# Attention and two mixtures of experts in one program: zero rows and expert weights issued at other steps, a first routing group of five tiles, k in 2 KB pieces, gates and domain probabilities made in the first mixture

## The chip, the cores and the metric

One Trainium2 chip, of which one core runs the whole program in a single launch. The core has five engines that run side by side, each with its own queue in order: TensorE (PE in the profile, PEld its weight loads), VectorE (DVE), ScalarE (ACT), GpSimd (POOL) and SyncE (SP), which here only issues DMAs. The metric is the device time of one execution in microseconds, lower is better. TensorE's granted clock in the profile is a share of 2.4 GHz, and 0.50 means 1.2 GHz.

## The reference, cut to what matters

```python
# attention: 4 batches, 8 heads, 576 positions, 64 wide; window of 128, linear bias by distance
scores = scale * np.matmul(q, k.transpose(0, 1, 3, 2))
scores = np.where((rel >= 0) & (rel < 128), scores + bias, -1e9)
attn = softmax(scores)                       # + 1e-9 in the denominator
x = (attn @ v) as 2304 rows of 512
# first mixture: 8 experts, each row goes to its best one alone
logits = x @ w_gate; e = argmax(logits)
gate = softmax(logits)[e]                    # + 1e-9 in the denominator
x = gate * (relu(x @ w1[e]) @ w2[e])
# second mixture: 4 domains, each row goes through all of them
p = domain_probs / (domain_probs.sum(-1) + 1e-9)
out = sum over e of p[:, e] * (relu(x @ w1[e]) @ w2[e])
```

## The kernel before, in words

The 2304 rows are 18 tiles of 128. Three stages follow one another: attention, the first mixture (one expert after the other, on the rows sorted by expert) and the second mixture (three passes over four domains). Nothing is scheduled by a planner: each engine's queue has the order in which the Python code is written.

**Attention** is a loop over 36 steps `s`, two per tile `t` (four heads each). It is a software pipeline: step `s` issues the scores of step s (`st_qk`, L419), the mask and maximum (`st_max`, on DVE), the exponentials of s-1 (`st_exp`, on ACT), the transposes of s-2 (`st_turn`, L463, copied out by ACT on L465), and the products with v of s-3 (`st_pv`, L486). Between the copy and the products POOL cuts each transposed block in two with two selects (L472): one for the tile's own keys and one for the tile before. `st_row` divides by the denominators on DVE and gives the finished rows `xrow` and the logits. The first steps of some tiles also turn a batch of v against the gate weights (`st_gates`, L554), which waits for `rvt`, v in transposed form.

**Routing** is done for groups of tiles (`CUTS`: 0-2, 3-5, 6-8, 9-11, 12-13, 14-15, 16, 17). When the last tile of a group is finished, the generator `st_route` takes the maximum, the one-hot choice `oh_all`, the rank of each row in its expert (matmuls into `rkp`, L630 to L636), and then one indirect DMA per tile on POOL's queue (L664), which scatters the rows into the DRAM table `xs`, at the place of their expert. `route_op` issues one operation of it at a time, three or four calls a step.

The table must be zero where no row lands. `clear_rows(e)` (L318) therefore writes 384 rows of zeros (768 KB) for each of the 8 experts, in the steps 2 to 9. A scatter can reach any of the 8 regions, so the first scatter waits for all of them.

**SP's queue** carries nearly all loads of this stage in one order: k, q and v of the next tiles (256 KB each; k and q three tiles ahead, v one), `rvt` in batches, the zero rows, and `raw`, the first weights of the first mixture (512 KB each). Six of these weights are already split into a high and a low part here (`w_split`: ACT makes `whi`, L146, and in the next step DVE makes `wlo`, L150), in the steps of `SPLITS`. The k tile in SBUF has the layout head pair, slot, column, so that one k tile lands in pieces of 512 bytes.

**Gates.** For all groups below `OPEN` (tile 14) the gate of each row is worked out beside the routing in attention (`gate_of`: a subtraction, an exponential on ACT, a sum, an addition, a reciprocal); for the last four tiles it is done in the first mixture by `places`, a generator that advances by one operation after each of the mixture's units from the second expert on. Its last product is `ct`, a table that the second mixture reads first. `domain_probs` (L389 to L392, four DVE operations) runs at step 20.

Of the kernel before, what the change touches and what calls it, by code (L numbers as in the profile page):

```python
# [19 lines left out]
P = 128  # L20
# [13 lines left out]
CUTS = 0, 3, 6, 9, 12, 14, 16, 17, 18  # L34
# [4 lines left out]
SPLITS = 6, 11, 16, 21, 26, 31  # L39
# [23 lines left out]
def kernel(  # L63
# [40 lines left out]
    lgl = const.tile([P, NTT - OPEN, E1], F32, tag="lgl", name="lgl")  # L104
    mxl = const.tile([P, NTT - OPEN, 1], F32, tag="mxl", name="mxl")
    shl = const.tile([P, NTT - OPEN, E1], F32, tag="shl", name="shl")
# [98 lines left out]
    def gate_of(t0, lg, mx, sh, apart=1):  # L205
        m = lg.shape[1]
        gs = gs_all[:, t0:t0 + m]
        nc.vector.tensor_tensor(out=sh, in0=lg, in1=mx.to_broadcast([P, m, E1]), op=ALU.subtract)
        for _ in range(apart):
            yield  # L210
        nc.scalar.activation(out=sh, in_=sh, func=AF.Exp)
        yield
        nc.vector.tensor_reduce(out=gs, in_=sh, axis=AX.X, op=ALU.add)
        yield
        nc.vector.tensor_scalar(out=gs, in0=gs, scalar1=1e-9, scalar2=None, op0=ALU.add)
        yield
        nc.vector.reciprocal(out=gs, in_=gs)
        yield

    def attention():  # L220
        actx = ExitStack()
        with actx:
# [12 lines left out]
            kr = c2.tile([P, NP, NK, P], F32, tag="kr", name="kr")  # L235
# [89 lines left out]
            dpt = c2.tile([P, N // P, E2], F32, tag="dpt", name="dpt")  # L325


# [11 lines left out]
            def row_consts():  # L339
                nc.sync.dma_start(out=dpt, in_=dp)  # L340
# [46 lines left out]
            def domain_probs():  # L387
                dsum = c2.tile([P, N // P, 1], F32, tag="dsum", name="dsum")
                nc.vector.tensor_reduce(out=dsum, in_=dpt, axis=AX.X, op=ALU.add)  # L389
                nc.vector.tensor_scalar(out=dsum, in0=dsum, scalar1=1e-9, scalar2=None, op0=ALU.add)  # L390
                nc.vector.reciprocal(out=dsum, in_=dsum)
                nc.vector.tensor_tensor(  # L392
                    out=pn, in0=dpt, in1=dsum.to_broadcast([P, N // P, E2]), op=ALU.mult
                )


# [13 lines left out]
            def st_qk(s):  # L410
                t, hf = divmod(s, 2)
                keys, sl = geom(t)
                w = len(keys) * P
                ps = ps_s.tile([P, 2, 2, 2 * P], F32, tag="sc", name=f"sc{s}")
                for jj in range(2):
                    j = 2 * hf + jj
                    for r in range(2):
                        rows = slice(r * D, (r + 1) * D)
                        nc.tensor.matmul(  # L419
                            ps[:, r, jj, 0:w], qs[t][rows, j, :], kr[rows, j, sl, :], start=True, stop=True  # L420
                        )
                sc[s] = ps
# [73 lines left out]
            def st_row(s):  # L496
# [3 lines left out]
                if hf == 0 and t < LATE:  # L500
                    rowt[t] = xpool.tile([P, H, D], F32, tag="row", name=f"xrow{t}", bufs=6)
# [80 lines left out]
            def st_logits(t):  # L582
                g = group_of[t]
                if t == groups[g][0]:
                    if t < OPEN:
                        lgs[g] = route.tile([P, len(groups[g]), E1], F32, tag="lg", name=f"lg{g}")
                    else:
                        lgs[g] = lgl[:, t - OPEN:t - OPEN + len(groups[g])]
# [5 lines left out]

            gates = []

            def st_route(g):
# [8 lines left out]
                mx = t3("mx", 1) if t0 < OPEN else mxl[:, t0 - OPEN:t0 - OPEN + m]  # L606
# [4 lines left out]
                if t0 < OPEN:  # L611
                    gates.append((g, gate_of(groups[g][0], lg, mx, t3("sh"), 4)))
# [130 lines left out]

            for s in range(ns):
# [4 lines left out]
                keep = st_gates(s - 2) if s == 2 else None  # L749
                closing = s == 2 * LATE + 3  # L750
# [19 lines left out]
                if s == 2:  # L770
                    nc.vector.tensor_tensor(
                        out=least, in0=fac, in1=small_of.to_broadcast([P, PER, H]), op=ALU.mult
                    )
                    st_vw(0)
                    st_last(0)
# [36 lines left out]
                while s == 2 * LATE + 2 and not waiting:  # L812
# [5 lines left out]
            for _, steps in gates:  # L818
                for _ in steps:
                    pass  # L820
# [14 lines left out]
    def moe():  # L835
        mctx = ExitStack()
        with mctx:
# [81 lines left out]
            def first_mixture():  # L919
                pctx = ExitStack()  # L920
                with pctx:
# [248 lines left out]

                    def places():
# [7 lines left out]
                        yield from gate_of(OPEN, lgl, mxl, shl)  # L1179
# [313 lines left out]
```

## Time and profile before

| what | time |
|---|---|
| three runs | 1143.1, 1146.97 and 1145.77 us, median 1145.77 us |
| the profiled execution | 1142.88 us |
| span of its instructions | 1141.2 us |
| TensorE busy in the span | 1122.5 us (98%) |
| VectorE, ScalarE, GpSimd busy | 764.6, 516.3, 117.4 us |
| mean granted clock | 0.996 |

The span begins and ends with TensorE's program, and the 1.7 us around it are start and end of the execution. A busy TensorE is not one at its peak: within attention its matmuls take turns with weight loads. So the time is read by stages. Step 0 of attention begins at 6.51 us of the span, step 35 at 135.69 us; the first matmul of the first mixture stands at 153.57 us.

### The profile page before, as it was taken

How to read it: one execution, taken by the hardware profiler on the slowest of the kernel's cores; microseconds unless marked ns; L12 is line 12 of the kernel's file. 1: busy time of each engine (PE TensorE's matmuls, PEld its weight loads, DVE VectorE, ACT ScalarE, POOL GpSimd, SP SyncE). 2: the span in 40 equal slices, each digit the busy share in tenths (PEclk: the TensorE clock that was granted, in tenths of full speed). 3: DMA queues.
4: the chain of work that ended last, by engine and by line, in shares of the span. 5: the costliest groups of instructions: out<-in, count | busy, mean ns of one | idle time of the engine just before them, and what ended most of it. 6: DMA issues, size and time to landing. Idle time of an engine off the chain costs nothing.

```text
span 1141.2 us, 17166 instructions
## 1 busy us (share of the span) xinstructions
PE 1122.5 (98%) x6490; PEld 1024.0 (90%) x6490; DVE 764.6 (67%) x1424; ACT 516.3 (45%) x1006; POOL 117.4 (10%) x192
## 2 busy tenths in 40 slices
PE   9899999999999999999999999999999999999997
PEld 6687889999999989999999999999999999999996
DVE  7778864645754686766667866666677966666663
ACT  6677734544654443344434433333334543433331
POOL 4444520012200000000000300000001100000002
PEclk9999999999999999999999999999999999999999
DMA  9966244555654122222121322211222312122201
GB/s 318 356 213 195 85 150 159 193 162 161 201 195 131 57 78 72 74 74 74 56 74 57 130 74 74 74 57 55 74 75 86 105 68 64 66 74 74 75 19 55
DMA packets 68941, 126.52 MB, mean 111 GB/s; under 512 B 26080, under 2 KB 35296, under 8 KB 68832
## 3 DMA queue, kind: packets, MB, share of 16 engines
q1 hardware_dynamic: 64544, 113.91, 31.1%
q0 software_dynamic: 3456, 9.51, 2.1%
q8 instruction: 76, 1.25, 0.4%
q10 hardware_dynamic: 832, 1.57, 0.4%
q14 instruction: 33, 0.27, 0.1%
HBM read 109.18 MB, written 15.80 MB: 110 GB/s over the span
## 4 chain that ended last, share of the span: by engine, by line
issue 71%; PE 12%; POOL 2%; POOLq 0%
PE y L972 6%; PE g L867 6%; POOL out_dram L1424 2%; PE xps L939 1%; POOLq L1489 0%; POOLq L1424 0%
## 5 line engine op out<-in xcount | busy, mean ns | idle before, releaser
L150 DVE TENSOR_TENSOR wlo<-raw,whi 128x1024 fp32r<-128x1024 f32 x160 | 193.7, 1223 | 128.9 <-ACT whi L146 127.5
L146 ACT CAST whi<-raw 128x1024 fp32r<-128x1024 f32 x160 | 165.7, 1055 | 134.2 <-DVE raw L172 111.1
L1399 PE MATMUL l<-whi,hlo 128*128 128x512 f32 x576 | 224.6, 390 | 0.0
L1399 PE MATMUL l<-wlo,hhi 128*128 128x512 f32 x576 | 224.5, 390 | 0.0
L1399 PE MATMUL l<-whi,hhi 128*128 128x512 f32 x576 | 224.0, 389 | 0.0
L1303 ACT COPY x<-X 128x384 f32<-128x384 f32 x126 | 60.7, 482 | 267.0 <-PE X L1282 267.0
L1420 DVE SCALAR_TENSOR_TENSOR acc<-l,ct,acc 128x512 f32<-128x512 f32 x126 | 94.2, 748 | 85.4 <-PE l L1399 85.4
L1399 PEld LDWEIGHTS l<-whi,hlo 128*128 128x128 f32 x576 | 108.1, 188 | 22.5
L1399 PEld LDWEIGHTS l<-wlo,hhi 128*128 128x128 f32 x576 | 108.1, 188 | 22.0
L1399 PEld LDWEIGHTS l<-whi,hhi 128*128 128x128 f32 x576 | 108.1, 188 | 21.9
L1424 POOL DMA_INDIRECT out_dram<-acc,ctok x18 | 23.3, 1294 | 812.5 <-DVE acc L1420 485.2
L1308 DVE TENSOR_TENSOR x<-Z,x 128x384 f32<-128x384 f32 x84 | 44.7, 553 | 67.6 <-ACT x L1303 67.6
L1314 ACT ACTIVATE hhi<-x 128x384 fp32r<-128x384 f32 x126 | 58.1, 521 | 30.9 <-DVE x L1308 30.9
L486 PE MATMUL xo<-vr,pt 128*128 128x104 f32 x448 | 66.2, 280 | 5.6 <-POOL pt L472 4.9
L972 PE MATMUL y<-hhi,whi 128*128 128x256 f32 (+2 forms) x224 | 69.5, 310 | 0.0
L972 PE MATMUL y<-hlo,whi 128*128 128x256 f32 (+2 forms) x224 | 69.0, 308 | 0.0
L972 PE MATMUL y<-hhi,wlo 128*128 128x256 f32 (+2 forms) x224 | 68.8, 307 | 0.0
L486 PEld LDWEIGHTS xo<-vr,pt 128*128 128x128 f32 x448 | 57.9, 194 | 10.7 <-POOL pt L472 6.4
L1320 DVE SCALAR_TENSOR_TENSOR hlo<-x,hhi 128x384 fp32r<-128x384 f32 x126 | 62.8, 553 | 2.8 <-ACT hhi L1314 0.2
L854 ACT ACTIVATE hhi<-g 128x384 fp32r<-128x384 f32 x64 | 31.3, 493 | 48.8 <-PE g L867 45.0
L855 DVE SCALAR_TENSOR_TENSOR hlo<-g,hhi 128x384 fp32r<-128x384 f32 x64 | 35.1, 554 | 26.7 <-ACT hhi L854 25.2
L472 POOL TENSOR_SCALAR_AFFINE_SELECT pt<-pt 128x512 f32<-128x512 f32 x64 | 40.9, 664 | 64.8 <-ACT pt L465 58.5
(362 smaller groups left out, 2496.9 us busy)
## 6 DMA issues: line engine op xcount, KB each, us to landing
raw<-in_w_b_dram SPq DMA_DIRECT2D x96, 512.0 KB, 3.4
raw<-in_w_a_dram SPq DMA_DIRECT2D x64, 512.0 KB, 3.7
xs<-zrow SPq DMA_DIRECT2D x8, 768.0 KB, 8.3
kr<-in_k_dram SPq DMA_DIRECT2D x18, 256.0 KB, 4.2
v<-in_v_dram SPq DMA_DIRECT2D x18, 256.0 KB, 5.2
row<-xs SPq DMA_DIRECT2D x6, 768.0 KB, 5.6
rq<-in_q_dram SPq DMA_DIRECT2D x16, 256.0 KB, 4.3
rvt<-in_vt_dram SPq DMA_DIRECT2D x3, 1024.0 KB
```

What stands on the lines that cost most here:

```text
L146: nc.scalar.copy(out=hi, in_=src)
L150: nc.vector.tensor_tensor(out=lo, in0=src, in1=hi.bitcast(F32), op=ALU.subtract)
L486: nc.tensor.matmul(xo[:, i, :], pt[c][:, i, :], rows[c % NV][:, h * span:h * span + WIDE], start=(n == 0), stop=(n == len(pt) - 1),)
L867: nc.tensor.matmul(ps[:, 0:w], wl[:, c0:c0 + P], xl[dt // 2][:, dt % 2, 0:w], start=(dt == 0 and n == 0), stop=(dt == NDT - 1 and n == 2),)
L972: nc.tensor.matmul(acc[:, 0:w], wl[:, c0:c0 + P], hl[:, 0:w], start=(f == 0 and x == 0), stop=(f == NFT - 1 and x == 2),)
L1303: nc.scalar.copy(out=to, in_=xb[i])
L1308: nc.vector.tensor_tensor(out=c, in0=ps, in1=c, op=ALU.add)
L1314: nc.scalar.activation(out=hi, in_=c, func=AF.Relu)
L1320: nc.vector.scalar_tensor_tensor(out=lo, in0=c, scalar=0.0, in1=hi.bitcast(F32), op0=ALU.max, op1=ALU.subtract)
L1399: nc.tensor.matmul(acc, hl[:, ts], wl[:, c0:c0 + DM], start=(m == 0 and x == 0), stop=(m == 3 and x == 2),)
L1420: nc.vector.scalar_tensor_tensor(out=accs[g], in0=acc, scalar=pe, in1=accs[g], op0=ALU.mult, op1=ALU.add)
L1424: nc.gpsimd.indirect_dma_start(out=outv[g], out_offset=bass.IndirectOffsetOnAxis(ap=ctok[:, g, :], axis=0), in_=accs.pop(g), in_offset=Non ...
```

## The change

The parts: `clear_rows` runs in the steps 2, 3, 5, 6, 8, 9, 11 and 12; the two weight loads of the steps 3 and 5 go to 10 and 12, and the six splits from the steps 6, 11, 16, 21, 26, 31 to 13, 16, 19, 22, 25, 28. The groups become 0-4, 5-7, 8-10, 11-12, 13-14, 15, 16, 17. The k tile's slot becomes the outer axis, so that a k tile lands in pieces of 2 KB. All gates and the domain probabilities are made in `places`. The gate columns of v of tile 0 (`st_vw(0)`) are issued after the scores of step 3.

```diff
-CUTS = 0, 3, 6, 9, 12, 14, 16, 17, 18
+CUTS = 0, 5, 8, 11, 13, 15, 16, 17, 18
-SPLITS = 6, 11, 16, 21, 26, 31
+SPLITS = 13, 16, 19, 22, 25, 28
-    lgl = const.tile([P, NTT - OPEN, E1], F32, tag="lgl", name="lgl")
+    lgl = const.tile([P, NTT, E1], F32, tag="lgl", name="lgl")
...
-    def gate_of(t0, lg, mx, sh, apart=1):
+    def gate_values():
+        gs, sh = gs_all, lgl
+        nc.vector.tensor_tensor(out=sh, in0=lgl, in1=mxl.to_broadcast([P, NTT, E1]), op=ALU.subtract)
+        yield
         nc.scalar.activation(out=sh, in_=sh, func=AF.Exp)
...
-            kr = c2.tile([P, NP, NK, P], F32, tag="kr", name="kr")
+            kr = c2.tile([P, NK, NP, P], F32, tag="kr", name="kr")
...
-                nc.sync.dma_start(out=kr[:, :, t % NK, :], in_=k[t])
+                nc.sync.dma_start(out=kr[:, t % NK], in_=k[t])
...
-                    rowt[t] = xpool.tile([P, H, D], F32, tag="row", name=f"xrow{t}", bufs=6)
+                    rowt[t] = xpool.tile([P, H, D], F32, tag="row", name=f"xrow{t}", bufs=8)
...
             def route_op(head=False):
-                if gates and not head and (waiting or not back):
-                    if next(gates[0][1], "end") == "end":
-                        gates.pop(0)
-                elif back and (head or not waiting):
+                if back and (head or not waiting):
...
+            clears = [2 + 3 * e // 2 for e in range(E1)]
             for s in range(ns):
...
+                if s == 3:
+                    st_vw(0)
+                    st_last(0)
...
-                if s in (3, 5):
+                if s in (SPLITS[0] - 3, SPLITS[0] - 1):
                     w_dma(nxt["dma"])
-                if 2 <= s < E1 + 2:
-                    clear_rows(s - 2)
-                if s == 20:
-                    domain_probs()
+                if s in clears:
+                    clear_rows(clears.index(s))
...
-                while s == 2 * LATE + 2 and not waiting:
+                while s >= 2 * LATE and back and not waiting:
                     route_op()
...
-                        yield from gate_of(OPEN, lgl, mxl, shl)
+                        yield from domain_probs()
+                        yield from gate_values()
```

Three places in the engines' queues show it. The first is where SP issues the last zero rows, and the loads in front of them. Before (`zrow` is the source of the zero rows, `rvt8` the batch of v from tile 8 on, the number of `rq` the tile):

```order
L318 DMA xs_69<-zrow_162 384x1x512
L258 DMA rvt8_693<-in_vt_dram 128x4x512
L318 DMA xs_69<-zrow_162 384x1x512
L249 DMA v1_0_126<-in_v_dram 128x8x64
L244 DMA kr_119<-in_k_dram 128x4x128
L245 DMA rq8_753<-in_q_dram 128x512
```

Now:

```order
L242 DMA rq8_717<-in_q_dram 128x512
L133 DMA raw0_720<-in_w_a_dram 128x1024
L315 DMA xs_69<-zrow_161 384x1x512
L246 DMA v1_1_126<-in_v_dram 128x8x64
L241 DMA kr_118<-in_k_dram 128x512
L242 DMA rq9_820<-in_q_dram 128x512
L133 DMA raw1_823<-in_w_a_dram 128x1024
L315 DMA xs_69<-zrow_161 384x1x512
```

The last zero rows stood before the q of tile 8 and stand now behind that of tile 9 and two weights.

The second is POOL's first scatter; `pt9` are the selects of step 9's probabilities, which step 11 issues. Before:

```order
L472 AFFINE_SELECT pt8_1_722<-pt8_718 128x512
L440 MEMSET pr11_762 128x4x64
L472 AFFINE_SELECT pt9_0_780<-pt9_778 128x512
L472 AFFINE_SELECT pt9_1_782<-pt9_778 128x512
L664 DMA xs_69<-xrow0_361,row_i_76 18433x512
L472 AFFINE_SELECT pt10_0_834<-pt10_832 128x512
```

Now:

```order
L456 AFFINE_SELECT pt12_1_902<-pt12_898 128x512
L456 AFFINE_SELECT pt13_0_963<-pt13_961 128x512
L456 AFFINE_SELECT pt13_1_965<-pt13_961 128x512
L641 DMA xs_69<-xrow0_359,row_i_76 18433x512
L456 AFFINE_SELECT pt14_0_1011<-pt14_1009 128x512
```

The first scatter moved four steps down POOL's queue.

The third is the end of POOL's queue in attention; the number of `xrow` is the tile. Before:

```order
L664 DMA xs_69<-xrow13_1776,row_i_76 18433x512
L472 AFFINE_SELECT pt33_0_2091<-pt33_2089 128x512
L472 AFFINE_SELECT pt33_1_2093<-pt33_2089 128x512
L664 DMA xs_69<-xrow14_1877,row_i_76 18433x512
L664 DMA xs_69<-xrow15_2000,row_i_76 18433x512
L472 AFFINE_SELECT pt34_0_2147<-pt34_2145 128x512
```

Now:

```order
L641 DMA xs_69<-xrow14_1836,row_i_76 18433x512
L456 AFFINE_SELECT pt33_0_2051<-pt33_2049 128x512
L456 AFFINE_SELECT pt33_1_2053<-pt33_2049 128x512
L641 DMA xs_69<-xrow15_1962,row_i_76 18433x512
L456 AFFINE_SELECT pt34_0_2103<-pt34_2101 128x512
```

Between the selects of the steps 33 and 34 stand one scatter now and two before.

## Rows read from the trace of the kernel before

**Rows 1.** Windows: stages; start and end, length, then busy time by engine.

```profile
core 0: us, PE busy (x) PEld busy (x) DVE busy (x) ACT busy (x) POOL busy (x), PEclk, DMA share, GB/s
25.07:48.18 23.11, 22.34 (x186) 18.51 (x186) 19.20 (x57) 17.95 (x56) 9.89 (x16) 1.00 1.04 360
48.18:57.36 9.18, 5.42 (x30) 4.46 (x29) 4.49 (x11) 3.22 (x11) 5.20 (x7) 0.84 1.07 321
57.36:135.69 78.33, 76.62 (x630) 63.28 (x629) 66.65 (x209) 59.29 (x182) 35.44 (x52) 1.00 0.55 172
...
159.41:400.00 240.59, 240.59 (x1651) 240.17 (x1652) 136.61 (x202) 122.17 (x198) 20.65 (x18) 1.00 0.49 157
```

**Rows 2.** Waits from 46 to 58 us: total, times, longest.

```profile
POOL xs L664 <- DMA kr<-in_k_dram: 5.7, 1, 5.7
...
PE xo L486 <- POOL pt L472: 3.6, 1, 3.6
```

**Rows 3.** Timeline, steps 13 and 14: start, length, engine, what; idle before.

```profile
48.18 1.13 PE L419 MATMUL sc<-kr,rq 64*128 64x256 f32 x8
...
51.78 1.16 POOL L664 DMA_INDIRECT xs<-xrow,row_i  x1 [5.69 <-DMA kr<-in_k_dram]
...
53.65 0.47 PE L486 MATMUL xo<-vr,pt 128*128 128x104 f32 x2 [3.64 <-POOL pt L472]
...
54.67 0.64 PE L486 MATMUL xo<-vr,pt 128*128 128x104 f32 x2
...
57.36 0.90 PE L419 MATMUL sc<-kr,rq 64*128 64x256 f32 x4
```

**Rows 4.** Zero rows: the last issue in the timeline, landing from line L318.

```profile
41.51 1.31 SPq L318 DMA_DIRECT2D xs<-zrow  x1
...
DMA to landing us min/median/max: 7.2/8.3/9.4
```

**Rows 5.** DMA of three windows: 1.9 to 51.8, 4.5 to 5.25, 6.75 to 7.5.

```profile
DMA packets 18928, 17.60 MB, mean 353 GB/s; under 512 B 8263, under 2 KB 12825, under 8 KB 18922
...
DMA packets 495, 0.23 MB, mean 311 GB/s; under 512 B 48, under 2 KB 495, under 8 KB 495
...
DMA packets 134, 0.27 MB, mean 366 GB/s; under 512 B 0, under 2 KB 0, under 8 KB 134
```

**Rows 6.** Timeline: steps 8 and 9, and the steps 24 and 25.

```profile
28.60 1.13 PE L419 MATMUL sc<-kr,rq 64*128 64x256 f32 x8
...
31.09 1.06 PE L554 MATMUL gates<-rvt,wbd 128*32 128x512 f32 x8 [0.77 <-DMA rvt<-in_vt_dram]
...
34.05 1.14 PE L419 MATMUL sc<-kr,rq 64*128 64x256 f32 x8
...
94.01 1.13 PE L419 MATMUL sc<-kr,rq 64*128 64x256 f32 x8
...
98.62 1.13 PE L419 MATMUL sc<-kr,rq 64*128 64x256 f32 x8
```

**Rows 7.** Timeline of POOL and PE behind step 35.

```profile
141.29 0.99 POOL L664 DMA_INDIRECT xs<-xrow,row_i  x1 [0.16 <-issue]
142.59 0.97 POOL L664 DMA_INDIRECT xs<-xrow,row_i  x1 [0.30 <-issue]
143.56 1.24 POOL L472 TENSOR_SCALAR_AFFINE_SELECT pt<-pt 128x512 f32<-128x512 f32 x2
...
144.27 0.47 PE L486 MATMUL xo<-vr,pt 128*128 128x104 f32 x2 [0.84 <-POOL pt L472]
```

**Rows 8.** Lines of the split up to 160 us; timeline of PE in step 29.

```profile
L150 DVE TENSOR_TENSOR wlo<-raw,whi x6: 1196/1219/1460, 29.6 to 130.0; 128x1024 fp32r<-128x1024 f32 x6
...
L146 ACT CAST whi<-raw x7: 1032/1047/1056, 25.7 to 159.5; 128x1024 fp32r<-128x1024 f32 x7
...
115.39 0.44 PE L486 MATMUL xo<-vr,pt 128*128 128x104 f32 x2 [0.53 <-DVE lgh L534]
```

**Rows 9.** Gate sums, a domain probability, and the table's first load and reader.

```profile
L213 DVE TENSOR_REDUCE gs_all<-sh x5: 157/169/169, 46.0 to 144.2; 128x3 f32<-128x24 f32 x4, 128x2 f32<-128x16 f32 x1
...
L389 DVE TENSOR_REDUCE dsum<-dpt x1: 219/219/219, 85.3 to 85.3; 128x18 f32<-128x72 f32 x1
...
L1418 DVE TENSOR_SCALAR acc<-l,ct x18: 744/745/751, 409.2 to 917.2; 128x512 f32<-128x512 f32 x18
L1207 SPq DMA_DIRECT2D ct<-ctab x1: 377/377/377, 306.6 to 306.6; - x1
```

More of the change, by code (lines that the diff above doesn't have):

```diff
@@ L103 @@
     off_i = const.tile([1, E1], I32, tag="off_i", name="off_i")
-    lgl = const.tile([P, NTT - OPEN, E1], F32, tag="lgl", name="lgl")
-    mxl = const.tile([P, NTT - OPEN, 1], F32, tag="mxl", name="mxl")
-    shl = const.tile([P, NTT - OPEN, E1], F32, tag="shl", name="shl")
+    lgl = const.tile([P, NTT, E1], F32, tag="lgl", name="lgl")
+    mxl = const.tile([P, NTT, 1], F32, tag="mxl", name="mxl")
     cnt_i = const.tile([1, E1], I32, tag="cnt_i", name="cnt_i")
@@ L203, in y_tile @@
         return (held if n < 5 else pools["yp"]).tile([P, DM], F32, tag=f"y{n}", name=name)
-    def gate_of(t0, lg, mx, sh, apart=1):
[L206 to L210, printed above, removed]
+    def gate_values():
+        gs, sh = gs_all, lgl
+        nc.vector.tensor_tensor(out=sh, in0=lgl, in1=mxl.to_broadcast([P, NTT, E1]), op=ALU.subtract)
+        yield
         nc.scalar.activation(out=sh, in_=sh, func=AF.Exp)
@@ L339, in row_consts @@
             def row_consts():
-                nc.sync.dma_start(out=dpt, in_=dp)
+                nc.sync.dma_start(out=pn, in_=dp)
             rc = {}
@@ L385, in late_consts @@
                 yield
[L387 to L394, printed above, removed]
             ns = 2 * NTT
@@ L419, in st_qk @@
                         nc.tensor.matmul(
-                            ps[:, r, jj, 0:w], qs[t][rows, j, :], kr[rows, j, sl, :], start=True, stop=True
+                            ps[:, r, jj, 0:w], qs[t][rows, j, :], kr[rows, sl, j, :], start=True, stop=True
                         )
@@ L584, in st_logits @@
                 if t == groups[g][0]:
[L585 to L588, printed above, removed]
+                    lgs[g] = lgl[:, t:t + len(groups[g])]
                 nc.vector.tensor_reduce(
@@ L593, in st_logits @@
                     back.append((g, st_route(g)))
-            gates = []
             def st_route(g):
@@ L604, in t3 @@
                     return route.tile([P, m, w], F32, tag=nm, name=f"{nm}{g}")
-                mx = t3("mx", 1) if t0 < OPEN else mxl[:, t0 - OPEN:t0 - OPEN + m]
+                mx = mxl[:, t0:t0 + m]
                 key, km, rk = t3("key"), t3("km", 1), t3("rk")
@@ L610, in st_route @@
                 nc.vector.tensor_reduce(out=mx, in_=lg, axis=AX.X, op=ALU.max)
-                if t0 < OPEN:
-                    gates.append((g, gate_of(groups[g][0], lg, mx, t3("sh"), 4)))
                 yield
@@ L773, in attention @@
                     )
-                    st_vw(0)
-                    st_last(0)
                 if hf == 1 and t:
@@ L817, in attention @@
             st_row(ns - 3)
-            for _, steps in gates:
-                for _ in steps:
-                    pass
             st_turn(ns - 1)
@@ L1168, in spill_chunk, with domain_probs @@
                             nc.vector.tensor_copy(out=tab[:, 0:NCH - 1], in_=rest)
+                    def domain_probs():
+                        dsum = sp.tile([P, N // P, 1], F32, tag="dsum", name="dsum")
+                        nc.vector.tensor_reduce(out=dsum, in_=pn, axis=AX.X, op=ALU.add)
+                        nc.vector.tensor_scalar(out=dsum, in0=dsum, scalar1=1e-9, scalar2=None, op0=ALU.add)
+                        yield
+                        nc.vector.reciprocal(out=dsum, in_=dsum)
+                        yield
+                        nc.vector.tensor_tensor(
+                            out=pn, in0=pn, in1=dsum.to_broadcast([P, N // P, E2]), op=ALU.mult
+                        )
+                        yield
                     def places():
```

1 line of the change is left out of this document (removed).

## The prediction, as made before the result was known

> **What bounds the kernel now.** The windows by stage come first [rows 1]. From 159.41 to 400 us TensorE is busy for all of 240.59 us, and VectorE for 136.61: in the mixtures TensorE sets the time, and small work added on VectorE or ScalarE has cover. In attention TensorE also leads (76.62 of 78.33 us between the steps 14 and 35), but VectorE follows close with 66.65 us, 85%. One stage is out of line: from the start of step 13 to that of step 14 pass 9.18 us, TensorE is busy for 5.42, the granted clock is 0.84 on the mean, and the DMA engines are full (1.07). The six steps before it took 23.11 us together; without step 8, treated below, five took 23.11 - 5.45 = 17.66, so 3.53 us each. That is the pace of an undisturbed step.
>
> The waits of that place say why [rows 2]: POOL's indirect DMA waited 5.7 us, and TensorE 3.6 us for POOL's selects. The profile puts POOL's wait down to a load of k, but a scatter reads no k. In the code the first scatter waits for the zero rows in all eight regions, so I take it for the last of these. The timeline is consistent with it [rows 3, 4]: the last zero rows are issued at 41.51 us, zero rows land 7.2 to 9.4 us after their issue, so at the latest near 50.9 to 52.2 us (counted from the issue's start or its end, 42.8), and the scatter starts at 51.78. POOL reached it at 51.78 - 5.69 = 46.09 us. The selects stand behind it in POOL's queue, the products with v need the selects, and so TensorE stood 3.64 us; the products after it took 0.64 us each pair, under a clock that had fallen from 2.4 to 1.2 GHz for part of this stage (1.00 to 0.84 on the mean, [rows 1]). Both losses lie inside the 9.18 us.
>
> **The change part by part.**
>
> *The scatter.* What must be moved before the last zero rows have landed? Before: k and q of eight tiles (16 x 0.262 MB), v of six (1.57), the transposed v of twelve (3.15), eight times zero rows (6.29), three weights (1.57), in all 16.8 MB; in the window 1.9 to 51.8 us 17.60 MB moved at 353 GB/s [rows 5], so the queue was full from the start and nearly all it carried stood ahead of the last zero rows. Now: k and q of ten tiles (5.24), v of eight (2.10), the same transposed v and zero rows, two weights (1.05): 17.8 MB. At 353 GB/s from 1.9 us this has landed at 1.9 + 50.5 = 52.4 us, hardly later than before. By the other way of counting, issue plus landing time: step 12 ends near 47.4 us now, and 9.4 us later is 56.8 us. But POOL reaches the first scatter four steps later: 46.09 + 4 x 3.53 - 0.8 (step 8, below) = 59.4 us. So the zero rows are there 2.6 to 7 us ahead, the wait goes, and step 13 falls from 9.18 to 3.53 us: **-5.65 us**. Were the wait not reduced at all it would be 0; both ends stay in the range. What is late next: v of tile 7, issued in front of the last zero rows, lands by 51 us at the rate above and is wanted in step 15, from 54 us on; k and q have three tiles of lead.
>
> *k in 2 KB pieces.* A window with nearly only 512 byte pieces moved 311 GB/s, one with 2 KB pieces alone 366 [rows 5]. For the ten k tiles ahead of the last zero rows (2.62 MB) that is 8.4 - 7.2 = 1.3 us of queue, which only widens the margin of the scatter; where nobody waits for a DMA it is worth nothing. I take 0 in the sum. The Trainium skill (DMA: Bandwidth & Descriptors, Specifications) has 512 bytes as the least transfer for line rate, so that by it even the 1.3 us would not be there and the margin would be that much smaller; the two windows above do not agree with it.
>
> *Step 8.* The product of v with the gate weights waited 0.77 us for its load, and the step took 34.05 - 28.60 = 5.45 us; step 24, with the same product and no such wait, took 98.62 - 94.01 = 4.61 [rows 6]. In SP's queue this load had three zero rows and a weight in front of it and now has two zero rows and no weight: 1.3 MB less, 3.7 us at 353 GB/s. The wait goes: **-0.84 us** (0 if another load fills the place).
>
> *The end of attention.* Behind step 35 POOL had two scatters in a row, 0.99 and 0.97 us, and behind them the selects for which TensorE stood 0.84 us [rows 7]. Now one scatter stands there, and the selects are free 1.3 us earlier (142.59 - 141.29): **-0.84 us**. Between 0 and 1.3 us, if the next wait behind it was nearly as late.
>
> *Splits closer together.* From step 13 to the end attention has six splits now and had four. Each is 1.05 us on ACT and 1.22 us on DVE [rows 8]. At nothing, if the engines' slack covers them; wholly on the path, two more cost 2 x 2.27 = 4.5 us. A split can reach TensorE: in step 29 it stood 0.53 us for VectorE, which was behind a split [rows 8]. But VectorE also gives work away in the same stretch: the four operations for domain probabilities, about 0.22 us each, and four of the gates, about 0.17 each, for four groups [rows 9], so 0.9 + 2.7 = 3.6 us against 2 x 1.22 = 2.4 us. The work is as much as before or a little less, and the stretch from step 14 on kept its 3.73 us a step (78.33 / 21) under it. I take 0, between -1.2 and +4.5 us.
>
> *Gates and probabilities in the first mixture.* They add some ten operations there, under TensorE's cover [rows 1], 0.2 to 0.3 us each: 0, at most 1 us if a few of them delay a hidden activation. Their chain grows by three calls; before, its table was loaded at 306.6 us and first read at 409.2 us [rows 9], and no unit takes as much as 100 us. Nothing waits.
>
> *Gate columns of tile 0 one step later.* The same instructions; 0, or 0.3 us either way.
>
> **Sum.** -5.65 - 0.84 - 0.84 = -7.33 us. The profiled execution took 1142.88 us (span 1141.2 and 1.7 around it) and becomes 1135.55. It was 2.9 us below the median of the runs, 1145.77; I forecast a median, so 1145.77 - 7.33 = **1138.4 us**.
>
> **The rivals.**
>
> *The zero rows are still late.* Then POOL waits in step 16 instead of step 12. For it: the last zero rows stand behind 1 MB more than before. Against it: the two counts above give 2.6 to 7 us of margin. It decides once they land behind 59.4 us; landing 3 us later than that returns 3 of the 5.65 us: 1141.4 us. The Trainium skill (DMA: Bandwidth & Descriptors, Queues, rings and completion order) says that a DMA engine consumes descriptors in ring order, so zero rows on SP's queue come after every load issued before them; the landing of 7.2 to 9.4 us for 768 KB agrees, since 768 KB alone would be 2.2 us at 353 GB/s.
>
> *The crowded splits eat most of it.* If each of the six costs about the 0.53 us seen once, and the work taken from VectorE was idle time anyway, 3.2 us come back; with the upper end of 4.5 us the gain is 2.8: 1141.6 to 1143 us. For it: VectorE is at 85% in this stretch, and in the steps 14, 20 and 26 a low part now falls together with the end of a group and the scaling of v. Against it: step 22 of before held the same combination.
>
> *Slower.* The same three steps, but with the clock. VectorE's work in each is about 5 us (66.65 / 21 = 3.2 of a mean step, a low part of 1.22, and the group's small operations, three or four of about 0.17 us [rows 1, 8, 9]), 1.5 us over the pace. If TensorE stands so long that its clock falls to 1.2 GHz as in rows 3, the rest of such a step takes double, 1.8 us more. Three steps at 3.3 us are 9.9 us, against -7.33: 1148.3 us. It decides from 2.4 us a step on. Against it: in the whole stretch of 78.33 us the granted clock was 1.00 [rows 1], through a step of that kind.
>
> **How the numbers follow.** Forecast 0.74, late zero rows 0.08, crowded splits 0.13, slower 0.04, and 0.01 for none of these. About 0.3%, 3.4 us, is what this kernel's measurement can tell from no change. The forecast and its own range, 1134 to 1141, lie below 1142.3; so does the late-zero case; half of the crowded one does not: faster 0.83, within 0.12, slower 0.05 (the last with a bad draw of runs, which spread over 3.9 us before). The range of 8 in 10 takes in both milder rivals: 1134 to 1143.
>
> **What would show it.** Right: no POOL wait over 1 us before a scatter, and none of TensorE for POOL's selects above 1 us between 45 and 70 us; step 13 at 3.4 to 3.7 us; a granted clock of 1.00 through attention; step 8 near 4.6 us; the first mixture's first matmul near 146.2 us in place of 153.57. Wrong: a scatter wait around 59 us; steps over 4.5 us after 14, 20 or 26 with TensorE waiting for VectorE's masks or denominators; or mixtures longer than before by over 1 us.

## The result and the profile after

The changed kernel takes 1134.28 us (median of 4 runs, 1133.36 to 1137.11), the kernel before 1146.07 beside it (4 runs, 1143.1 to 1146.97). The medians lie 11.8 us apart. The ratio of the means is 0.9906, with a 95% interval of 0.9879 to 0.9932: 10.8 us less, between 7.8 and 13.9. Forecast were 1138.4 us with a range of 1134 to 1143, so the direction held, and the result lies 4 us below the forecast, just inside the range. The profiled executions went from 1142.88 to 1133.38 us, the spans from 1141.2 to 1131.7.

The windows of the changed kernel by stage answer to [rows 1]; columns as there. They are step 7 to the start of step 13, step 13, the steps 14 to 34, step 35 to the first mixture's first matmul, and a stretch of the mixture.

```profile
23.90:45.93 22.03, 22.03 (x181) 18.16 (x180) 16.59 (x45) 16.02 (x53) 8.90 (x16) 1.00 1.08 384
45.93:49.45 3.52, 3.52 (x30) 3.05 (x29) 3.17 (x11) 3.07 (x11) 1.22 (x2) 1.00 1.07 394
49.45:127.45 78.00, 76.28 (x637) 63.40 (x637) 68.52 (x200) 60.48 (x182) 40.47 (x57) 1.00 0.64 200
127.45:143.96 16.51, 15.73 (x127) 14.37 (x126) 13.49 (x60) 7.73 (x23) 9.47 (x13) 1.00 0.31 112
159.41:400.00 240.59, 240.59 (x1646) 239.29 (x1645) 141.59 (x215) 123.71 (x202) 19.68 (x18) 1.00 0.47 155
```

The step that took 9.18 us takes 3.52, TensorE has no gap from step 7 up to step 14, and the granted clock is 1.00 in every stage. The DMA engines are as full as before (1.07). In the mixture VectorE has 5 us more work (141.59 against 136.61) and TensorE still has no gap.

The last zero rows, the selects and the first scatter, from the timelines of SP and POOL (start, length, engine, what; idle before), answer to [rows 3, 4]:

```profile
44.62 0.53 SPq L315 DMA_DIRECT2D xs<-zrow  x1
...
56.90 1.22 POOL L456 TENSOR_SCALAR_AFFINE_SELECT pt<-pt 128x512 f32<-128x512 f32 x2 [2.50 <-ACT pt L449]
58.30 1.16 POOL L641 DMA_INDIRECT xs<-xrow,row_i  x1 [0.17 <-DVE den L497]
```

The scatter waits 0.17 us, not 5.69. Of the zero rows the trace resolves one landing, that of the sixth of the eight regions, issued at 31.41 us: it took 10.0 us. If the last takes as long, it lands at 54.6 us, 3.5 us before POOL gets to the scatter (58.30 - 0.17 = 58.13).

Step 8 on TensorE answers to [rows 6]:

```profile
27.43 1.13 PE L403 MATMUL sc<-kr,rq 64*128 64x256 f32 x8
...
29.08 1.07 PE L538 MATMUL gates<-rvt,wbd 128*32 128x512 f32 x8
30.08 2.03 PE L470 MATMUL xo<-vr,pt 128*128 128x104 f32 x16
32.04 0.49 PE L403 MATMUL sc<-kr,rq 64*128 64x256 f32 x2
```

The product with the gate weights waits for nothing, and the step takes 32.04 - 27.43 = 4.61 us. At the end of attention (timelines of POOL and of TensorE) one scatter stands between the selects of two steps, and the products with v no longer wait 0.84 us as in [rows 7]:

```profile
132.86 0.99 POOL L641 DMA_INDIRECT xs<-xrow,row_i  x1 [0.16 <-issue]
133.86 1.33 POOL L456 TENSOR_SCALAR_AFFINE_SELECT pt<-pt 128x512 f32<-128x512 f32 x2
...
134.84 0.37 PE L470 MATMUL xo<-vr,pt 128*128 128x104 f32 x2
```

Stage by stage, from the first matmul of each step, the 9.6 us by which the first matmul of the first mixture comes earlier (153.57 to 143.96) are: start of step 0 -1.11, steps 0 to 7 -0.06, step 8 -0.84, steps 9 to 12 -0.24, step 13 -5.65, steps 14 to 34 -0.33, step 35 to the first mixture -1.37. The mixtures take 0.1 us more.

### The profile page after: what moved, and what is told of

The parts are those of the page before. It is cut to its first block, busy times and chain, and to the rows that moved or that the text cites. A ratio compares the mean times of both kernels' runs of the same rounds, so it can differ in the third digit from the quotient of the medians.

```text
span 1131.7 us, 17141 instructions
## 1 busy us (share of the span) xinstructions
PE 1118.3 (99%) x6490; PEld 1021.7 (90%) x6490; DVE 762.8 (67%) x1403; ACT 515.0 (46%) x1001; POOL 115.8 (10%) x192
## 3 DMA queue, kind: packets, MB, share of 16 engines
q10 hardware_dynamic: 832, 1.57, 0.4%
## 4 chain that ended last, share of the span: by engine, by line
issue 43%; PE 41%; POOL 2%; DVE 1%; POOLq 0%; ACT 0%
PE l L1383 10%; PE g L838 10%; PE y L943 9%; PE X L1266 6%; PE Z L1266 3%; POOL out_dram L1408 2%; PE Y L1266 1%; PE y L954 1%; PE xps L910 1%; DVE hlo L1304 0%; POOLq L1473 0%; DVE x L1292 0%; POOLq L1408 0%; DVE acc L1404 0%; ACT hhi L1298 0%
## 5 line engine op out<-in xcount | busy, mean ns | idle before, releaser
L437 ACT ACTIVATE pr<-pr,nm 128x128 f32<-128x128 f32 x144 | 46.0, 390 | 1.7
```

The source lines that it names most:

```text
L437: nc.scalar.activation(out=pr[:, r, jj, :], in_=pr[:, r, jj, :], func=AF.Exp, bias=nm[:, r, jj:jj + 1], scale=0.125,)
```

## The same kernels once more: what one profile hides

Both kernels were profiled a second time, unchanged. What each theory expected of the kernel before:

> The kernel before, profiled once more. Theory A (the start of step 0 is a draw of the execution that follows the first rise of the clock): step 0 begins anywhere from 5.3 to 6.6 us, within 0.3 us of where other kernels with the same rise began (rise near 4.0 to 4.5 us: 5.3 to 5.65; rise at 6.0 to 7.0: 6.3 to 6.5). Theory B (the kernel sets it): 6.5 us again, within 0.15. Both: step 8 at 5.4 to 5.9, step 13 near 9.2 us, and if the start is early, step 8 or step 13 longer by about as much, since the loads' landing stays.

and of the changed one:

> The changed kernel, profiled once more. Theory A (a draw): step 0 begins between 5.3 and 6.6 us as the clock's first rise has it. Theory B (the kernel sets it): 5.4 us again, within 0.15. Both: step 8 at 4.61 and step 13 at 3.53, steps 14 to 35 at 78.0 us within 0.2, step 35 to the first mixture matmul 16.5 us.

The first rows of TensorE's timeline are the twelve warm-up matmuls, behind which step 0 stands. In the kernel before, the first profile, and in its second:

```profile
1.28 5.30 PE L116 MATMUL idle<-idle 128*128 128x512 bf16 x12 [1.28 <-DVE idle L260]
```

```profile
1.28 4.16 PE L116 MATMUL idle<-idle 128*128 128x512 bf16 x12 [1.28 <-DVE idle L260]
```

The same twelve matmuls took 5.30 and 4.16 us, and step 0 began at 6.51 and 5.36 us. In the changed kernel they took 4.19 and 4.38 us, and step 0 began at 5.40 and 5.59. Of thirteen profiles with twelve of them, of whichever kernel, twelve have step 0 begin when they are done; in the one with the new groups alone it waited 0.20 us more for k. The profile's clock column reads 1.00 from the start here, but the pace of the matmuls tells more: in the first profile they start some 0.43 us apart to the last, and in the second the last five start 0.22 us apart, twice the pace, as between 1.2 and 2.4 GHz. I take it from this that the clock rises at another moment in each execution of one program; the 1.11 us at the start are then a draw, not the change. The Trainium skill (TensorE: Matmul & The Clock Gate, What's actually happening) says that the number of matmuls before the clock rises varies from run to run of the same kernel; 5.30 against 4.16 us agrees.

That the start is a draw is what theory A had for both kernels (5.59 us lies 0.19 from the changed kernel's first 5.40, little more than theory B's 0.15). What both theories had for the rest held in the changed kernel but not in the kernel before: step 8 took 6.12 us, not up to 5.9, and step 13 took 11.11 (47.96 to 59.07), not 9.2. So the 1.15 us of earlier start were lost more than three times over. Windows of its second profile: step 8; steps 13 and 14 together; the steps 15 to 34; step 35 to the mixture.

```profile
27.70:33.82 6.12, 4.68 (x37) 3.15 (x36) 3.62 (x9) 3.97 (x13) 4.46 (x6) 1.00 1.03 346
47.96:63.93 15.97, 10.51 (x58) 8.71 (x57) 6.76 (x17) 5.90 (x21) 5.79 (x8) 0.68 0.90 277
63.93:138.60 74.67, 72.97 (x602) 60.15 (x601) 64.32 (x203) 56.43 (x174) 34.80 (x51) 1.00 0.53 163
138.60:156.47 17.87, 16.16 (x128) 14.42 (x127) 14.12 (x65) 7.89 (x24) 10.44 (x14) 1.00 0.32 118
```

The same two steps in its first profile:

```profile
48.18:60.98 12.80, 9.04 (x58) 7.59 (x58) 6.77 (x17) 5.42 (x18) 5.57 (x7) 0.87 1.07 328
```

The steps 13 and 14 took 15.97 us in place of 12.80. In the second profile POOL's first scatter waited 7.5 us (from its timeline, and TensorE's):

```profile
53.37 1.16 POOL L664 DMA_INDIRECT xs<-xrow,row_i  x1 [7.51 <-DMA kr<-in_k_dram]
...
55.25 0.75 PE L486 MATMUL xo<-vr,pt 128*128 128x104 f32 x2 [5.46 <-POOL pt L472]
```

It was reached 0.2 us earlier and released 1.6 us later than in [rows 3]; TensorE stood 5.46 in place of 3.64 us. The mean clock of 0.68 over 15.97 us is 2 x 0.32 x 15.97 = 10.2 us at 1.2 GHz, where the first profile had 2 x 0.13 x 12.80 = 3.3. So the same wait costs 5.5 us in one execution (12.80 - 7.25, the changed kernel's steps 13 and 14) and 8.7 in another. Why the release came 1.6 us later is not shown: the last zero rows were issued at 42.04 us, only 0.5 us later than in the first profile. The changed kernel's windows in its second profile: step 8, step 13, steps 14 to 34, step 35 to the mixture.

```profile
27.69:32.30 4.61, 4.61 (x37) 3.13 (x37) 2.34 (x7) 3.50 (x12) 2.58 (x5) 1.00 1.11 373
46.19:49.72 3.53, 3.53 (x31) 3.05 (x30) 3.18 (x11) 3.08 (x11) 1.23 (x2) 1.00 1.06 379
49.72:127.73 78.01, 76.27 (x638) 63.40 (x637) 68.56 (x201) 60.48 (x182) 40.52 (x57) 1.00 0.63 201
127.73:144.27 16.54, 15.82 (x127) 14.37 (x126) 13.51 (x60) 7.73 (x23) 9.49 (x13) 1.00 0.30 112
```

Those are the first profile's numbers again, to 0.03 us. Second against second, the first mixture matmul goes from 156.47 to 144.27 us, and the times from 1146.02 to 1133.66: -12.4 us, against -9.5 from the first pair. The runs' medians lie between (-11.8).

## The experiments

All are single runs with a profile. The kernel before was run three more times beside them: with the first four kernels it took 1146.42 us, with those from k in 512 byte pieces to the old steps of zero rows, weights and splits 1141.80, and with the rest and the second profiles 1144.33. Its own times thus spread over 5 us, so the experiments are read by their steps and not by their times. Numbers are from the first matmul of each step; "tail" is from step 35 to the first mixture's first matmul. The last column is the time.

| kernel | step 0 at | step 8 | steps 13, 14 | steps 15-34 | tail | mixture at | us |
|---|---|---|---|---|---|---|---|
| before, first / second | 6.51 / 5.36 | 5.45 / 6.12 | 12.80 / 15.97 | 74.71 / 74.67 | 17.88 / 17.87 | 153.57 / 156.47 | 1142.88 / 1146.02 |
| after, first / second | 5.40 / 5.59 | 4.61 / 4.61 | 7.25 / 7.25 | 74.27 / 74.29 | 16.51 / 16.54 | 143.96 / 144.27 | 1133.38 / 1133.66 |

The kernels below stand with the steps that differ.

**Only the groups** (and the loop that issues the end of the routing):

```diff
-CUTS = 0, 3, 6, 9, 12, 14, 16, 17, 18
+CUTS = 0, 5, 8, 11, 13, 15, 16, 17, 18
-while s == 2 * LATE + 2 and not waiting:
+while s >= 2 * LATE and back and not waiting:
-... name=f"xrow{t}", bufs=6)
+... name=f"xrow{t}", bufs=8)
```

> Before, with the new groups alone (and the two rows of buffers and the loop at the end that they need); zero rows, weights, k and gates as before. Theory: the later first scatter is what removes the wait. Zero rows land near 51.8 us as before, the scatter is reached four steps later near 60 us: step 13 at 3.5 us in place of 9.18, no POOL wait over 1 us before a scatter; step 8 stays at 5.45 us; from step 35 to the first matmul of the mixture 16.5 us in place of 17.88, since one scatter less stands before the selects of step 34. First matmul of the mixture at 146.5 us (start at 6.5). Rival: the wait comes from the crowded DMA queue, and goes only with the zero rows spread; then step 13 or a step up to 17 keeps 3 to 6 us of it.

1143.71 us. Step 13 takes 3.53 us and the first scatter finds its zero rows (POOL's timeline): the groups alone remove the wait.

```profile
64.44 1.16 POOL L664 DMA_INDIRECT xs<-xrow,row_i  x1 [0.17 <-DVE lgh L534]
```

But what was won there is lost again in two other places. The first is step 8, which takes 10.28 us and not the 5.45 expected (TensorE's timeline):

```profile
28.86 0.66 PE L463 MATMUL pt<-ident,pr 128*128 128x128 f32 x4
32.54 1.94 PE L554 MATMUL gates<-rvt,wbd 128*32 128x512 f32 x8 [3.02 <-DMA rvt<-in_vt_dram]
34.41 3.75 PE L486 MATMUL xo<-vr,pt 128*128 128x104 f32 x16
```

Step 0 began at 5.65 us here, so step 8 came 0.80 us earlier than in the first profile of before, the load was there 1.45 us later, and TensorE waited 3.02 us. What stood behind the wait ran at 1.2 GHz: the products took 3.75 us in place of 2.03. The second place is the steps 14 to 34, which take 81.28 us in place of 78.33: step 33 alone takes 6.69 (4.50 in the changed kernel), since the rank waits 1.47 us there for the one-hot choice on VectorE and 3.4 us at 1.2 GHz follow. The kernel with the splits at their old steps, below, has the same wait. In the tail the gate sums still stand beside the routing, and the rank of the late group waited for VectorE (timelines of TensorE and of VectorE):

```profile
146.31 0.31 PE L630 MATMUL rkp<-base,top 128*128 128x16 f32 x2
147.90 0.17 PE L634 MATMUL rkp<-oh_all,tri 128*128 128x16 bf16 x1 [1.28 <-DVE oh_all L625]
```

```profile
145.18 0.16 DVE L213 TENSOR_REDUCE gs_all<-sh 128x2 f32<-128x16 f32 x1
...
146.59 0.14 DVE L610 TENSOR_REDUCE mxl<-lgl 128x1 f32<-128x8 f32 x1
...
147.49 0.36 DVE L625 TENSOR_TENSOR oh_all<-key,km 128x8 bf16<-128x8 f32 x1
```

Seven gate operations stand on VectorE from 145.18 to 146.59 us, ahead of the maximum from which the one-hot choice follows. From step 35 (136.87) to that first rank matmul pass 9.44 us, as in the changed kernel (136.89 - 127.45), against 10.81 before: the groups give 1.37 us there. The 1.28 us of wait take them back, and the tail is 17.77.

**Only the zero rows and weights spread out:**

```diff
-SPLITS = 6, 11, 16, 21, 26, 31
+SPLITS = 13, 16, 19, 22, 25, 28
-if s in (3, 5):
+if s in (SPLITS[0] - 3, SPLITS[0] - 1):
     w_dma(nxt["dma"])
-if 2 <= s < E1 + 2:
-    clear_rows(s - 2)
+if s in clears:
+    clear_rows(clears.index(s))
```

With the old groups some zero rows are issued behind the first scatters here, so rows scattered early into the regions of the last two experts can be zeroed again and are missing from the output.

> Before, with only the zero rows and the weights spread over later steps; groups, k and gates as before. Theory: this part alone does nothing for the scatter: it is reached near 45 us and the last zero rows land at 52 to 54 us, so POOL waits 7 to 9 us, more than before, and step 13 takes 9 to 12 us; step 8 falls to 4.61 us. Rival: spreading empties the queue, the zero rows land earlier than 50 us and the wait shrinks below 4 us.

1149.04 us. Step 8 is at 4.61 us as expected, and step 13 at 3.53, not at 9 to 12: the first scatter does not wait, and the next two do (POOL's timeline):

```profile
45.26 1.16 POOL L664 DMA_INDIRECT xs<-xrow,row_i  x1 [0.17 <-DVE gs_all L215]
...
53.51 0.98 POOL L664 DMA_INDIRECT xs<-xrow,row_i  x1 [4.69 <-DMA xs<-zrow]
...
62.44 0.98 POOL L664 DMA_INDIRECT xs<-xrow,row_i  x1 [6.70 <-DMA xs<-zrow]
```

Here the profile names the zero rows themselves as what a scatter waits for. They are the two that stand behind the first scatter and were issued only at 48.61 and 57.50 us, so this kernel shows zero rows and scatters taking turns, and not how long a first scatter would wait for spread zero rows. The steps 14 to 16 take 23.53 us.

**Only k in 2 KB pieces:**

```diff
-kr = c2.tile([P, NP, NK, P], F32, tag="kr", name="kr")
+kr = c2.tile([P, NK, NP, P], F32, tag="kr", name="kr")
-nc.sync.dma_start(out=kr[:, :, t % NK, :], in_=k[t])
+nc.sync.dma_start(out=kr[:, t % NK], in_=k[t])
```

> Before, with only k in 2 KB pieces. Theory: eight k tiles are ahead of the last zero rows, 1.0 us of queue at 311 and 366 GB/s, so POOL's wait falls from 5.7 to 4.5 us and step 13 to about 8 us; step 8 loses up to its 0.8 us. Step 0 begins where the clock of the warm-up matmuls puts it, between 5.4 and 6.6 us, whatever the pieces. Rival: the pieces are worth nothing (512 bytes are enough), wait 5.7 us, step 8 at 5.45 us. Second rival, for the start: step 0 waits for the first k, and with 2 KB pieces it begins near 5.4 us.

1142.27 us. Step 0 at 5.30, step 8 at 5.16 us with a wait of 0.48 for its load, step 13 8.75 and the steps 13 and 14 13.68 us; the scatter still waited:

```profile
49.67 1.16 POOL L664 DMA_INDIRECT xs<-xrow,row_i  x1 [5.14 <-DMA kr<-in_k_dram]
```

It was released at 49.67 us, where the two profiles of before had 51.78 and 53.37 and the next kernel, with pieces of 512 bytes too, 52.49: the pieces bring the zero rows forward by some 2 us or more, and do not remove the wait.

**Only the gates and probabilities moved:** the changed kernel with the other three parts undone (groups, spreading and k pieces as in the diffs above, reversed). The gate columns of tile 0 stay behind the scores of step 3, and the new loop at the end stays too.

> Before, with only the gates and domain probabilities moved into the first mixture (and the loop at the end of the new kernel); groups, zero rows, weights and k as before. Theory: nothing on the path: scatter wait 5.7 us, step 8 5.45 us; steps 14 to 35 78.3 us in place of 78.33, within 0.6; step 35 to the mixture 17.6 to 17.9 us. Rival: VectorE bounds the late steps, and without 3.6 us of its work steps 14 to 35 take 75 to 77 us.

1141.84 us. Step 8 waits 1.92 us and takes 8.02, with the clock at 1.2 GHz behind the wait (0.81 on the mean of the step); step 13, reached later for it, takes 6.55, and its scatter waits 3.96. The steps 15 to 34 take 74.06 us in place of 74.71 and 74.67, and the tail stays at 17.91. By themselves the gates bring 0.6 us, less than the 1.3 us or more of the rival. The steps 2 and 3 take 6.45 us together, 6.46 before, so where the gate columns of tile 0 stand costs nothing.

**The changed kernel with k in 512 byte pieces** (the third diff reversed):

> The changed kernel with the old k layout (512 byte pieces). Theory: k's pieces only lengthen the DMA queue, by 1.3 us up to the last zero rows; the scatter has more margin than that, so steps 8 to 16 read as in the changed kernel (4.6, 3.5 and so on, no POOL wait over 1 us). Step 0 begins where TensorE's clock puts it: 5.6 us if the clock rises near 4.2 us, 6.3 to 6.5 us if near 6.2 us. Rival: the 2 KB pieces make the start and the end of the step 8 wait; then step 0 begins at 6.5 us whenever the clock rises, and step 8 takes over 5 us.

1134.75 us. Step 0 began at 6.51 us; step 8 (4.61), step 13 (3.53), steps 14 to 34 (78.02) and the tail (16.54) are those of the changed kernel. Given the rest, the pieces are worth nothing in time. What they do to the queue shows in the issue of the last zero rows (SP's timeline), which in the kernel with two scatters ahead of the last selects, below, stands at 45.24 us with 2 KB pieces and the same start of 6.51:

```profile
47.97 0.60 SPq L315 DMA_DIRECT2D xs<-zrow  x1
```

That is 2.7 us, more than the 1.3 expected.

**The changed kernel with six warm-up matmuls:**

```diff
-busy(ps_t, "t", 12)
+busy(ps_t, "t", 6)
```

> The changed kernel with 6 in place of 12 warm-up matmuls. Theory: step 0 waits for the warm-up matmuls, not for k: it begins when q and k have landed, near 4.5 us, and everything behind it moves forward by 0.5 to 1 us against a start of 5.4 (1.5 to 2 us against one of 6.5), as long as the clock rises all the same. Rival: fewer matmuls before step 0 delay the rise of the clock, the first steps run at 1.2 GHz, and step 4 begins no earlier than in the changed kernel (13.5 us).

1135.84 us. Step 0 began at 4.79 us, but at the pace of 1.2 GHz (its scores took 2.08 us, 1.16 in the changed kernel), and step 4 at 14.08 (13.47 and 13.74 in the changed kernel). The start is not to be had by a shorter warm-up. The first mixture came at 144.56 us, only 0.6 later than in the changed kernel's first profile; the other 1.9 us lie in the mixtures, where TensorE once stood 1.74 us for nothing that the profile shows. All other profiles have 987.4 to 987.8 us for the mixtures.

**The changed kernel with two scatters ahead of the last selects again:**

```diff
-CUTS = 0, 5, 8, 11, 13, 15, 16, 17, 18
+CUTS = 0, 5, 8, 11, 12, 14, 16, 17, 18
```

> The changed kernel with the groups 0-4, 5-7, 8-10, 11, 12-13, 14-15, 16, 17: again two scatters in a row before the selects of step 34. Theory: from step 35 to the first matmul of the mixture 17.7 us in place of 16.51, TensorE standing near 0.8 to 1.2 us for POOL's selects. Rival: the 1.4 us came from the gate operations that left VectorE's queue there; then it stays at 16.5 to 16.8 us.

1137.02 us, and a tail of 19.13, longer than before the change (17.88). TensorE's timeline:

```profile
137.17 0.47 PE L470 MATMUL xo<-vr,pt 128*128 128x104 f32 x2 [0.83 <-POOL pt L456]
...
144.03 0.66 PE L664 MATMUL xps<-ident,early 128*128 128x128 f32 x4 [1.54 <-DMA early<-xs]
```

The 0.83 us for the selects came back as expected; the tail is longer than either theory had. The second wait was not expected: the load that fetches the first sorted rows is issued 2.9 us behind the last scatter ahead of it (138.36 behind 135.49 us, and in the changed kernel 135.75 behind 132.86), so a later scatter holds it up.

**The changed kernel with zero rows, weights and splits at the old steps** (the second diff reversed), and then **with the zero rows alone at the old steps**:

```diff
-if s in clears:
-    clear_rows(clears.index(s))
+if 2 <= s < E1 + 2:
+    clear_rows(s - 2)
```

> The changed kernel with the zero rows and weights at their old steps; groups, k pieces and gates as in the changed kernel. Theory: the scatter still finds its zero rows (step 13 at 3.5 us), but the gate columns of step 8 wait again for v, as with the new groups alone: step 8 takes 5.2 to 10 us, the upper end where TensorE's clock falls. Rival: the 2 KB pieces alone make that load early enough; step 8 takes 4.6 us and attention is as short as in the changed kernel.

> The changed kernel with the zero rows back at the steps 2 to 9 and the splits and their weights at the new steps. Theory A (the later splits cost the 1.6 us when both were put back): steps 14 to 35 at 78.0 us, no scatter wait, step 8 at 4.6, step 13 at 3.5, so every step from 3 on as in the changed kernel. Theory B (the zero rows' place cost it): steps 14 to 35 near 79.5 us. Either way step 2 to 4 may be up to 0.8 us longer, since the zero rows again stand in front of the next loads.

1135.6 and 1134.52 us. Step 8 takes 4.61 in both, step 13 3.53; the wait that the theory had in step 8 did not come. Windows of step 8 and of the steps 14 to 34, of the first:

```profile
28.22:32.83 4.61, 4.61 (x37) 3.13 (x37) 3.40 (x9) 3.87 (x13) 3.56 (x5) 1.00 1.08 379
50.24:129.81 79.57, 76.71 (x637) 63.48 (x636) 67.45 (x200) 58.59 (x180) 41.99 (x57) 1.00 0.60 191
```

and of the second:

```profile
28.73:33.34 4.61, 4.61 (x38) 3.13 (x37) 2.33 (x7) 3.50 (x12) 2.58 (x5) 1.00 1.09 383
50.75:128.75 78.00, 76.28 (x638) 63.40 (x637) 68.52 (x201) 60.45 (x182) 40.42 (x57) 1.00 0.63 196
```

So the 1.57 us that the first loses between the steps 14 and 34 belong to the splits' place and not to that of the zero rows. Its waits of TensorE there (total, times, longest):

```profile
PE rkp L611 <- DVE oh_all L602: 1.5, 1, 1.5
PE xo L470 <- POOL pt L456: 0.8, 1, 0.8
```

The low part that the old places make in step 32 fits the first: it stands on VectorE (1.22 us from 122.38) ahead of the one-hot choice (124.13) for which step 33 waits, and that step took 5.48 us against 4.50. The second wait is in step 28, 4.46 us against 3.42; what made the selects late there is not shown. The steps 22 and 23 are 0.46 us shorter. With the zero rows early, the steps 2 and 3 took 7.28 us against 6.44 and 6.52, as the last expectation allowed: the next loads stand behind them. Their last issue is at 35.57 us, against 44.62 with the spread.

**The changed kernel with a first group of four tiles:**

```diff
-CUTS = 0, 5, 8, 11, 13, 15, 16, 17, 18
+CUTS = 0, 4, 8, 11, 13, 15, 16, 17, 18
```

> The changed kernel with a first group of four tiles in place of five (groups 0-3, 4-7, then as changed). POOL reaches the first scatter two steps earlier, near 51 us. Theory A (the zero rows land about 10 us after the last issue at 44.62 us, near 54.6): POOL waits 3 to 4 us there, TensorE 1.5 to 3 us for the selects behind it, the clock falls for a few us, and the steps 11 to 14 are 2.5 to 6 us longer together; first mixture matmul at 146.5 to 150 us if step 0 begins at 5.4. Theory B (the margin is larger than the landing suggests, the queue has them in place by 51 us): no wait over 1 us, every step within 0.3 us of the changed kernel.

1134.42 us. POOL's and TensorE's timelines:

```profile
53.39 1.16 POOL L641 DMA_INDIRECT xs<-xrow,row_i  x1 [2.12 <-DVE nm L429]
...
56.85 0.47 PE L470 MATMUL xo<-vl,pt 128*128 128x104 f32 x2 [1.11 <-POOL pt L456]
```

The wait is 2.1 us, less than theory A's 3 to 4 and more than theory B's 1; TensorE stood 1.28 us in two pieces (0.17 and 1.11), step 15 (not 11 to 14) grew by 1.8 us, the clock stayed at 1.00, and the first mixture matmul came 1.1 us later than in the changed kernel. The profile names a maximum on VectorE, which a scatter does not read; zero rows issued at 44.97 us and landing 8.4 us later fit (this run's landings took 7.6 to 10.4), but that is inferred. The margin of the changed kernel is then about 3.5 to 5 us, the one by the landing of 10.0 us and the other by 8.4.

No kernel here is faster than the changed one beyond what a single run can tell.

## Why the prediction was right and where it was short

**The scatter.** Right, with its mechanism: step 13 went from 9.18 to 3.53 us as written. POOL got to the scatter at 58.13 us; 59.4 was forecast, from a start of step 0 that was 1.11 us later. The margin of 2.6 to 7 us was some 3.5 to 5, by landings of 10.0 and 8.4 us. It is the first group of five that does it: alone it removes the wait, and a group of four brings 2.12 us of it back. The spreading of the zero rows, which the prediction weighed only as a risk, works against it, since it puts the last issue 9 us later (44.62 against 35.57 us), and is affordable because of the group. In no trace did a transfer on SP's queue land before one issued ahead of it, as far as landings are resolved.

**Where the forecast was short.** Of the 4.2 us between the forecast (1138.44 before rounding) and 1134.28, 2.2 lie in the profiled execution: from it alone 1135.55 us was forecast and 1133.38 measured. Half of that, 1.1 us, is luck, the draw at the start; 0.5 are the end of attention, below, and the rest is spread over the other steps. The other 2.0 lie in the step from the profile to the median: "It was 2.9 us below the median of the runs, 1145.77; I forecast a median, so 1145.77 - 7.33." That treats the gap between an execution and the median as a constant that both kernels share, and the changed kernel's profile was only 0.9 us below its own median. The second profile of before, at 1146.02 us, shows one way in which such a gap arises: it lies in the very waits that go, since the steps 13 and 14 were 3.2 us longer and step 8 0.7. In that execution the change takes 8.7 us at the scatter and 1.5 at step 8, not 5.65 and 0.84. It is one execution: a run of before at 1141.80 us has no trace, and neither have those of the changed kernel at 1135.18 and 1137.11, so what spreads the runs besides these waits stays open.

**Step 8.** The number was exact, 4.61 us, and the reason given holds. With the zero rows and weights spread alone, the load of v was issued at 18.40 us and landed at 26.3, 3.8 us before TensorE turned it; in the second profile of before it was issued at 21.40 and landed at 30.73, and TensorE had waited 1.44 us for it. The 2 KB pieces help in part: alone they left a wait of 0.48 us in a step 8 that began at 27.33 us. With them and the old places of the zero rows there was no wait either, but step 8 began later there (28.22 and 28.73 us), so that the pieces suffice is not shown. With neither, both ends of the wait vary: 0.77, 1.44, 1.92 and 3.02 us in four executions, step 8 beginning between 27.70 and 28.60 us and the load there between 30.86 and 32.54.

**k in 2 KB pieces** were taken at 0 with 1.3 us of margin. Given the other parts the 0 holds. The margin was mis-sized: the last zero rows were issued 2.7 us earlier with the pieces (45.24 against 47.97 us), and alone the pieces moved the scatter's release by some 2 us or more. The Trainium skill (DMA: Bandwidth & Descriptors, Specifications) has 512 bytes as enough for line rate; the kernel that changes only the pieces, with its release at 49.67 against 51.78, 53.37 and 52.49 us, speaks against it, as far as four executions can.

**The end of attention** was mis-sized: -0.84 forecast, -1.37 and -1.33 measured in the two pairs of profiles. One scatter fewer gives the 1.37 up to the first rank matmul (0.84 of it the wait), but it is kept only because the gate sums are gone from VectorE there: with the groups alone 1.28 us came back as a wait for the one-hot choice. The gates were costed at 0 and were, given the new groups, worth that much.

**The splits** cost nothing, net of what the gates give back, by standing closer (78.00 us for 21 steps, 78.33 before), so the crowded rival and the slower one are out; the clock was 1.00 in the steps 14, 20 and 26. The prediction counted the gates of four groups as work that leaves this stretch; only three groups have all of theirs in it before the change, and of a fourth one operation, so VectorE lost 0.9 + 2.2 us there and not 3.6, still more than the 2.4 of two low parts. What the prediction did not see is that the splits' old places would have cost 1.57 us under the new groups, and 3.3 with the old gates, zero rows and pieces as well (81.28 - 78.00), where the clock fell too.

**The mixtures** took 987.71 us against 987.60, as forecast. The gate columns of tile 0 cost nothing, as forecast: the steps 0 to 7 took 22.03 us, and 22.09 before.

## What to carry to other kernels

Before a sum taken from one profile is set against a median, compare the profile's time with the runs: where it lies low, the waits that a change removes may be larger in a usual run, and a second profile of the same kernel shows whether they are. Where work ahead of a load gets faster or starts earlier, the wait for that load can grow, and the clock that falls behind it adds to the loss: with the new groups alone this took back most of the scatter's gain at step 8. A part of a change can lose elsewhere what it wins until another part stands beside it, as the groups did until the splits and the gates had moved, so undo single parts from the changed kernel as well as adding single parts to the one before.

## What was not expected of the hardware

One program begins its first useful step up to 1.15 us earlier or later, as the clock rises early or late in its warm-up (twelve matmuls in 4.16 or 5.30 us). And a wait's price depends on the clock behind it: 3.02 us of standing in step 8 made the step 5.7 us longer (10.28 against 4.61), since the rest of it ran at 1.2 GHz, while 1.28 us in the kernel with four tiles left the clock at 1.00 and made the steps up to the mixture 1.1 us longer. The length of the wait alone does not settle it: in step 33 a wait of 1.47 us was followed by 3.4 us at 1.2 GHz in the kernel with the new groups alone (step 33 at 6.69 us, mean clock 0.81), and one of 1.48 us for the same operation left the clock at 1.00 in the kernel with the splits at their old steps (5.48 us). In the kernel before, a wait of 3.64 us brought 3.3 us at 1.2 GHz in one execution and one of 5.46 us brought 10.2 in another.
